# A ring of eight x buffers, three weighting buffers and PSUM sums in the column loop of a long convolution with expert choice

## The chip, the cores and the metric

The kernel runs on one core of a Trainium2 chip. The metric is the device time of one execution in microseconds, the median of several runs.

## The reference

The first part is a long causal convolution per channel, computed by a discrete Fourier transform of length 2S; the second gives 128 tokens of each batch to a small two-layer network.

```python
B, S, D = 4, 12608, 128
h = (maximum(pos_emb @ w1, 0) @ w2) * exp(-0.01 * arange(S))[:, None]
u = x * v
y = irfft(rfft(u, 2*S, axis=1) * rfft(h, 2*S, axis=0), 2*S, axis=1)[:, :S]
a = x * y                                        # (B, S, D)
scores = einsum('bsd,d->bs', a, w_gate)
out = a.copy()
for b in range(B):
    idx = argpartition(-scores[b], 128)[:128]    # the 128 largest scores
    ye = maximum(a[b, idx] @ moe_w1, 0) @ moe_w2 # D -> 1024 -> D
    out[b, idx] += sigmoid(scores[b, idx])[:, None] * ye
```

## The kernel before

**Pipeline.** The transform of length 23114 = 91 x 254 is done by matmuls in stages. For each batch there are 32 groups of four channels; one iteration `t` of the main loop (line 1093) works on one group in several stages of delay: `load_u` and `load_h` (SyncE) load its inputs, `stage_u` (GpSimd, line 262) forms x * v, `f_s1` and `dft` (TensorE, lines 450 and 281) transform it, with copies by ScalarE (line 452 to `te`, line 284 to `qs`), `f_v`, `f_u`, `f_m`, `f_y` (VectorE, lines 456 to 471) multiply the spectra, `f_sd` (GpSimd) folds, and three iterations later `f_i` (TensorE, line 276) transforms half way back; ScalarE copies its result to `big` (lines 501, 502). Each engine works through its instructions in the order in which the program issues them, and all ordinary DMAs go through SyncE's one queue in that order. Waits are put in where two instructions touch the same data.

**Column loop.** When all 32 groups of a batch are in `big`, `P1.run` (line 632) makes the outputs of that batch: 127 columns of 128 positions by 128 channels, in 16 blocks of up to 8 columns, in the order `ORD`. i is a block's place in that order. A block is two half-blocks of four columns, h = 0 to 31. For each half-block:

- `mm` (lines 567, 571): TensorE makes four columns of the convolution in one PSUM bank, from a ring of four.
- `fin` (line 582): VectorE multiplies them with the block's x and writes the result over x, in SBUF.
- `weigh` (line 616): the result times the gate weights goes to a buffer ("room") of 4 x 128 columns. Half-blocks of the far blocks are weighted by GpSimd in two rooms of its own (`CE`), the other 20 by VectorE in rooms taken in turn. The weights for VectorE are a copy in the first bank of `bank2[1]`.
- `sums` (line 626): ScalarE sums each column of a room with a copy in place and an accumulator; this is the gate score. The sums of h >= 28 are left for later, except in the last batch.
- After the second half: the block's result is stored to HBM from the buffer of x (line 605), and the next x is loaded (line 544) into the buffer of the block before this one, whose store must have landed.

The buffers of x are seven places of 8 x 128 columns, block i in place i % 7. Places 0 to 4 are `xa` buffers, loaded in halves during the last groups of the batch (`LA`, line 1154). Places 5 and 6 are `XE[0]` and `XE[1]`, which lie over buffers of the pipeline that are idle during the loop; they are loaded at the loop's start (line 640). `XE[0]` begins at `qs` and covers both `qs` buffers and part of `mt`; `XE[1]` lies over `ws` and the start of the first `yz` buffer. The rooms of VectorE are two `wx` buffers, an idle `te` buffer and an idle `ht` buffer (`sd` in the last loop).

After the loop `f_i` and `dft` of the next iteration run; `dft` ends with ScalarE's copy to `qs`, and ScalarE's copies for `te` come right behind it. The selection of the 128 tokens (`topk_one`) runs in hooks of the next batch's iterations. After the fourth loop nothing covers it: the last selection and the last expert run follow.

Before the first loop the `xa` buffers are cleared by ScalarE, two in each of the first iterations (line 1111), since rows of x outside the sequence are not loaded. `gap` (line 209) is room at the end of PSUM banks for masks and small results.

Of the kernel before, what the change touches and what calls it, by code (L numbers as in the profile page):

```python
# [11 lines left out]
AF = mybir.ActivationFunctionType  # L12
# [5 lines left out]
B, S, D, FO = 4, 12608, 128, 64  # L18
# [5 lines left out]
NG = 32  # L24
HC = 4 * N1
# [4 lines left out]
HB = 4  # L30
# [7 lines left out]
NU, NV, NX, NH = 4, 2, 5, 3  # L38
# [2 lines left out]
PJ = (N3 + 1) // 2  # L41
NC, CO = 4, 2
NE = 3
LA = range(32 - 12, 32 - 2)
NS, ND = 66, 4
NWARM = 8
JB = 9
# [7 lines left out]
OFF, _o = {}, 0  # L55
# [3 lines left out]
    _o += _k * _w  # L59
ARENA = _o  # L60
XE = [OFF["qs"][0] + k * 12 * D for k in range(2)]
CE = [o + 8 * D for o in XE]
POS0, HID0 = 0, PJ * N1

# [109 lines left out]
def hyena_moe(ctx, tc, xg, x2, pos, bw, ww, wg, mw1, mw2, fo, fc, c1, gx, cf, ci, wm, tk, out):  # L174
# [18 lines left out]
    def buf(name, k, shape):  # L193
        o, n, w = OFF[name]
        return view(arena, o + (k + (name == "yz")) % n * w, shape)
# [11 lines left out]
        return view(bank2[k], 0, shape)  # L207

    def gap(k, n):
        return bank2[k].rearrange("p (c x) -> p c x", c=2)[:, :, HC:HC + n]  # L210

    def c3(a):
        return a.rearrange("p (c x) -> p c x", c=2)
# [312 lines left out]
    class P1:  # L526
# [10 lines left out]
        def load_a(self, i, a=0, z=8):  # L537
            if i < len(ORD):
                k = ORD[i]
                j0, j1 = blocks[k]  # L540
                z = min(z, j1 - j0)
                o = i % (NX + len(XE))
                self.xa[k] = buf("xa", o, [128, 8, D]) if o < NX else view(arena, XE[o - NX], [128, 8, D])
                nc.sync.dma_start(self.xa[k][P0:P0 + PR, a:z], x2[self.b, :, j0 + a:j0 + z])

        def comb(self):
# [27 lines left out]
        def fin(self, h):  # L574
            ja, n = self.hbs[h]
            blk = ja // 8
            xa = self.xa[blk]
            js = slice(ja % 8, ja % 8 + n)
            end = self.last and h >= len(self.hbs) - 2
            if end:  # L580
                self.weigh()
            nc.vector.tensor_tensor(out=xa[:, js], in0=self.s4.pop(h)[:, :n], in1=xa[:, js], op=ALU.mult)  # L582
            if not end:
                self.weigh()
                far = ja >= JM and h + 1 < len(self.hbs) and h not in DW
                if h >= NL and not self.last:
                    o = OFF["cm"][0] + 2 * NC * D if h < 30 else OFF["wx"][0]
                    wx = view(arena, o + h % 2 * HB * D, [128, HB, D])
                elif far:
                    wx = view(arena, CE[self.pw % 2], [128, HB, D])  # L590
                    self.pw += 1
                else:
                    wx = view(arena, self.wx[self.nw % 4], [128, HB, D])
                    self.nw += 1
                self.mul = xa[:, js], wx[:, :n], ja, n, far, h
                if far:
                    self.weigh()
            else:
                for k in range(n):
                    nc.vector.scalar_tensor_tensor(out=junk, in0=xa[:, ja % 8 + k], scalar=1.0,  # L600
                                                   in1=self.wg, op0=ALU.mult, op1=ALU.mult,
                                                   accum_out=self.sc[:, ja + k:ja + k + 1])
            if ja + n == blocks[blk][1]:
                j0, j1 = blocks[blk]
                nc.sync.dma_start(out[self.b, :, j0:j1], xa[P0:P0 + PR, :j1 - j0])
                i = ORD.index(blk)
                if i:
                    self.load_a(i - 1 + NX + len(XE))
                if blk in CB:
                    self.comb()  # L610

        def weigh(self):
            if self.mul:
                x, wx, ja, n, far, h = self.mul
                eng, w = (nc.gpsimd, wgb) if far else (nc.vector, self.wg)
                eng.tensor_tensor(out=wx, in0=x, in1=w.unsqueeze(1).to_broadcast([128, n, D]), op=ALU.mult)  # L616
                cols = [(wx[:, k], ja + k) for k in range(n)]
                if h < NL or self.last:
                    self.sums(cols)
                else:  # L620
                    self.late += cols
            self.mul = None

        def sums(self, cols):
            for x, j in cols:
                nc.scalar.activation(out=x, in_=x, func=AF.Copy, accum_out=self.sc[:, j:j + 1])  # L626

        def mask(self):
            sc, m = (self.sc, negm) if self.last else (c3(self.sc), negp)
# [2 lines left out]
        def run(self, ex):  # L632
            self.last = ex is not None
            self.ring = (0, 1, 2) if ex else (3, 2, 0, 1)
            self.wx = [OFF["wx"][0], OFF["wx"][0] + HB * D, OFF["te"][0] + (2 * HC if ex else 0),
                       OFF["sd"][0] if ex else OFF["ht"][0] + ((self.b + 1) * NG + 2) % NH * 2 * HC]
            self.wg = ps2(1, [128, D], f"wg_{self.b}")
            nc.scalar.copy(out=self.wg, in_=wgb)
            for k in range(len(XE)):
                self.load_a(NX + k)  # L640
            for k in range(2):
                self.comb()
            for h in range(len(self.hbs)):
# [449 lines left out]
    for t in range(NT + LAG):  # L1093
# [4 lines left out]
        if t < NT:  # L1098
# [9 lines left out]
            spare[0] = None  # L1108
            bg.hook("w", 1)
            load_u(t + NU)  # L1110
            for k in range(2 * t, min(2 * t + 2, NX)):
                nc.scalar.activation(out=buf("xa", k, [128, 8 * D]), in_=one.to_broadcast([128, 8 * D]), func=AF.Copy,
                                     scale=0.0)
            if t == 2:
                nc.scalar.copy(out=negp, in_=c3(negm))
# [99 lines left out]
```

## Time and profile before

| | us |
|---|---|
| median of 3 runs (lowest, highest) | 869.85 (867.72, 872.17) |
| the profiled execution | 872.12 |
| its span, first to last instruction | 870.3 |
| TensorE matmuls busy in it | 833.4 (96%) |
| VectorE busy | 750.5 (86%) |
| GpSimd busy | 720.1 (83%) |
| ScalarE busy | 626.3 (72%) |

The granted TensorE clock is 0.99 of full speed. Busy shares are means over stages with different limits: a wait counts where it is the last to end. In the rows PE is TensorE, DVE VectorE, ACT ScalarE, POOL GpSimd, SP SyncE; `a` and `c` are PSUM banks, `arena` the SBUF area of most buffers, `big` the transformed groups, `out_dram` the output.

### The profile page before, as it was taken

How to read it: one execution, taken by the hardware profiler on the slowest of the kernel's cores; microseconds unless marked ns; L12 is line 12 of the kernel's file. 1: busy time of each engine (PE TensorE's matmuls, PEld its weight loads, DVE VectorE, ACT ScalarE, POOL GpSimd, SP SyncE). 2: the span in 40 equal slices, each digit the busy share in tenths (PEclk: the TensorE clock that was granted, in tenths of full speed). 3: DMA queues.
4: the chain of work that ended last, by engine and by line, in shares of the span. 5: the costliest groups of instructions: out<-in, count | busy, mean ns of one | idle time of the engine just before them, and what ended most of it. 6: DMA issues, size and time to landing. Idle time of an engine off the chain costs nothing.

```text
span 870.3 us, 45948 instructions
## 1 busy us (share of the span) xinstructions
PE 833.4 (96%) x19382; PEld 684.6 (79%) x19382; DVE 750.5 (86%) x1498; ACT 626.3 (72%) x2291; POOL 720.1 (83%) x837
## 2 busy tenths in 40 slices
PE   8999999999999999999998999999999999999875
PEld 5766668888889777778897777778996777779864
DVE  7978789999999799999996998999978989997873
ACT  6665575555559879885597898965797989657961
POOL 5799659999999689998997798989977989889610
PEclk9999999999999999999999999999999999999987
DMA  7044587677878977688789767788788767857810
GB/s 255 9 168 173 189 296 235 219 220 233 273 224 277 310 215 214 210 235 253 229 242 298 243 202 221 225 257 249 207 278 284 216 198 237 239 153 211 297 45 7
DMA packets 83278, 190.32 MB, mean 219 GB/s; under 512 B 9699, under 2 KB 46668, under 8 KB 83072
## 3 DMA queue, kind: packets, MB, share of 16 engines
q1 hardware_dynamic: 82816, 186.86, 68.5%
q8 instruction: 152, 2.49, 1.2%
q0 software_dynamic: 256, 0.52, 0.2%
q14 instruction: 54, 0.44, 0.1%
HBM read 147.63 MB, written 39.71 MB: 215 GB/s over the span
## 4 chain that ended last, share of the span: by engine, by line
PE 71%; DVE 14%; DMA 7%; ACT 5%; issue 2%; POOL 0%; POOLq 0%; DVEq 0%; ACTq 0%; SPq 0%
PE c L276 20%; PE c L281 15%; PE a L450 15%; DMA out_dram<-arena 5%; ACT arena L626 3%; PE c L571 3%; PE a L567 3%; PE a L397 3%; PE c L397 2%; PE a L571 2%; PE c L422 2%; PE c L567 2%; DVE big L365 2%; DMA arena<-in_x_dram 2%; DVE arena L464 1%
## 5 line engine op out<-in xcount | busy, mean ns | idle before, releaser
L276 PE MATMUL c<-ci_sb,arena 128*23 128x128 f32 x8128 | 250.0, 273 | 6.6 <-issue 3.2
L276 PEld LDWEIGHTS c<-ci_sb,arena 128*23 128x23 f32 x8128 | 227.7, 103 | 16.3 <-issue 7.0
L281 PE MATMUL c<-arena,cf_sb 128*32 128x364 f32 x2048 | 183.5, 470 | 7.0 <-ACT arena L452 4.6
L450 PE MATMUL a<-cons,arena 128*32 128x182 f32 (+1 forms) x4096 | 185.5, 318 | 0.7 <-DVE arena L582 0.5
L450 PEld LDWEIGHTS a<-cons,arena 128*32 128x32 f32 (+1 forms) x4096 | 137.2, 110 | 45.1 <-issue 11.2
L501 ACT COPY big<-c 128x800 f32<-128x800 f32 x127 | 103.8, 818 | 81.8 <-PE c L276 81.4
L626 ACT ACTIVATE arena<-arena 128x128 f32<-128x128 f32 x504 | 148.0, 299 | 11.5 <-DVE arena L616 11.4
L477 POOL TENSOR_TENSOR arena<-arena 128x364 f32<-128x364 f32 x127 | 113.8, 896 | 49.4 <-DVE arena L471 41.4
L452 ACT COPY arena<-a 128x364 f32<-128x364 f32 x256 | 119.5, 467 | 42.1 <-PE a L450 36.9
L262 POOL TENSOR_TENSOR arena<-arena 128x508 f32<-128x508 f32 x128 | 139.1, 1087 | 9.0 <-DMA arena<-in_xg_dram 9.0
L464 DVE TENSOR_TENSOR arena<-c,arena 128x728 f32<-128x728 f32 x127 | 116.3, 915 | 3.8
L465 DVE TENSOR_TENSOR c<-c,arena 128x728 f32<-128x728 f32 x127 | 116.1, 915 | 0.0
L478 POOL TENSOR_TENSOR arena<-arena 128x364 f32<-128x364 f32 x127 | 114.3, 900 | 0.0
L281 PEld LDWEIGHTS c<-arena,cf_sb 128*32 128x32 f32 x2048 | 69.3, 110 | 52.5 <-issue 31.6
L626 ACT ACTIVATION_READ_ACCUMULATOR arena<-arena 128x1 f32 x504 | 96.3, 191 | 0.0
L459 DVE TENSOR_TENSOR c<-c,arena 128x364 f32<-128x364 f32 x128 | 69.6, 544 | 23.6 <-ACT arena L284 21.0
L521 POOL TENSOR_TENSOR big<-big,arena 128x224 f32<-128x224 f32 x128 | 74.4, 581 | 10.0
L554 POOL TENSOR_TENSOR arena<-big 128x512 f32<-128x512 f32 x64 | 80.0, 1284 | 0.7 <-PE a L567 0.3
L470 DVE TENSOR_TENSOR arena<-c,arena 128x364 f32<-128x364 f32 x127 | 68.3, 537 | 12.8
L284 ACT COPY arena<-c 128x364 f32<-128x364 f32 x128 | 59.1, 462 | 26.1 <-DMA out_dram<-arena 9.1
L520 POOL TENSOR_TENSOR big<-big,arena 128x224 f32<-128x224 f32 x128 | 74.5, 582 | 0.0
L456 DVE TENSOR_TENSOR c<-c,arena 128x364 f32<-128x364 f32 x128 | 69.6, 544 | 2.6
(222 smaller groups left out, 1374.0 us busy)
## 6 DMA issues: line engine op xcount, KB each, us to landing
arena<-in_xg_dram SPq DMA_DIRECT2D x256, 254.0 KB, 3.5
arena<-hd SPq DMA_DIRECT2D x128, 364.0 KB, 4.2
out_dram<-arena SPq DMA_DIRECT2D x64, 420.0 KB, 6.0
arena<-in_x_dram SPq DMA_DIRECT2D x44, 420.0 KB, 5.0
hd<-arena SPq DMA_DIRECT2D x32, 364.0 KB, 2.4
arena<-in_x_dram SPq DMA_DIRECT2D x40, 210.0 KB, 4.8
arena<-in_pos_dram SPq DMA_DIRECT2D x16, 182.0 KB, 3.9
arena<-in_moe_w_dram SPq DMA_DIRECT2D x2, 512.0 KB, 6.0
```

What stands on the lines that cost most here:

```text
L262: nc.gpsimd.tensor_tensor(out=x, in0=x, in1=v, op=ALU.mult)
L276: nc.tensor.matmul(o[32 * k:32 * k + c.stop - c.start], lhsT=lhsT[:, c], rhs=rhs, start=True, stop=True)
L281: nc.tensor.matmul(pq[w][a:a + 32], lhsT=cf_sb[:, 2 * w + a // NQ, a % NQ:a % NQ + 32], rhs=te[:, a // NQ], start=True, stop=True)
L450: nc.tensor.matmul(tps[s // 2][c, s % 2], lhsT=u[:, s, c], rhs=c1_sb[:, k], start=True, stop=True)
L452: nc.scalar.copy(out=te[:, :, 2 * h:2 * h + 2].rearrange("p e s i -> p s e i"), in_=tps[h])
L464: nc.vector.tensor_tensor(out=mt, in0=uv, in1=ht[:, 0].unsqueeze(1).to_broadcast([128, 2, HC]), op=ALU.mult)
L465: nc.vector.tensor_tensor(out=uv, in0=uv, in1=ht[:, 1].unsqueeze(1).to_broadcast([128, 2, HC]), op=ALU.mult)
L477: eng.tensor_tensor(out=nat(sd[:, 0]), in0=nat(yz[:, 0]), in1=rev(yz[:, 1]), op=ALU.add)
L478: eng.tensor_tensor(out=nat(sd[:, 1]), in0=rev(yz[:, 0]), in1=nat(yz[:, 1]), op=ALU.subtract)
L501: nc.scalar.copy(out=ay[:, t % NG, :NJ + JM, ss], in_=o3[:, :, :NJ + JM].rearrange("p s x -> p x s"))
L554: nc.gpsimd.tensor_tensor(out=cm[:, e].rearrange("p j (g s) -> p j g s", s=4), in0=av[0], in1=av[1], op=op)
L626: nc.scalar.activation(out=x, in_=x, func=AF.Copy, accum_out=self.sc[:, j:j + 1])
```

## The change

Places: an eighth one is added, over the two `wx` buffers, and comes first in the list `XP`; the `xa` buffers follow, then `XE[0]` and `XE[1]`. The first six are loaded in halves during the last groups, two iterations earlier than before, and are cleared at the start. VectorE's rooms are now three: the idle `te` buffer, the second bank of `bank2[1]` in PSUM, and the idle `ht` (or `sd`) buffer. The sums over the room in PSUM write their products to a piece of SBUF behind the `te` room. To free that bank, the gaps are contiguous columns of the first bank.

```diff
-LA = range(32 - 12, 32 - 2)
+LA = range(32 - 14, 32 - 2)
...
+XP = [OFF["wx"][0], *(OFF["xa"][0] + k * 8 * D for k in range(NX)), *XE]
+NP0 = NX + 1
...
     def gap(k, n):
-        return bank2[k].rearrange("p (c x) -> p c x", c=2)[:, :, HC:HC + n]
+        return bank2[k][:, HC:HC + 2 * n].rearrange("p (c x) -> p c x", c=2)
...
-                o = i % (NX + len(XE))
-                self.xa[k] = buf("xa", o, [128, 8, D]) if o < NX else view(arena, XE[o - NX], [128, 8, D])
+                self.xa[k] = view(arena, XP[i % len(XP)], [128, 8, D])
...
-                    wx = view(arena, self.wx[self.nw % 4], [128, HB, D])
+                    wx = self.wx[self.nw % 3]
...
                 if i:
-                    self.load_a(i - 1 + NX + len(XE))
+                    self.load_a(i - 1 + len(XP))
...
-                cols = [(wx[:, k], ja + k) for k in range(n)]
+                cols = [(wx[:, k], wx[:, k] if wx.tensor is arena.tensor else self.sums_o, ja + k) for k in range(n)]
...
-            for x, j in cols:
-                nc.scalar.activation(out=x, in_=x, func=AF.Copy, accum_out=self.sc[:, j:j + 1])
+            for x, o, j in cols:
+                nc.scalar.activation(out=o, in_=x, func=AF.Copy, accum_out=self.sc[:, j:j + 1])
...
-            self.wx = [OFF["wx"][0], OFF["wx"][0] + HB * D, OFF["te"][0] + (2 * HC if ex else 0),
-                       OFF["sd"][0] if ex else OFF["ht"][0] + ((self.b + 1) * NG + 2) % NH * 2 * HC]
+            o = OFF["te"][0] + (2 * HC if ex else 0), OFF["sd"][0] if ex else OFF["ht"][0] + ((self.b + 1) * NG + 2) % NH * 2 * HC
+            self.wx = [view(arena, o[0], [128, HB, D]), view(bank2[1], 512, [128, HB, D]), view(arena, o[1], [128, HB, D])]
+            self.sums_o = view(arena, o[0] + HB * D, [128, D])
...
             for k in range(len(XE)):
-                self.load_a(NX + k)
+                self.load_a(NP0 + k)
...
-            for k in range(2 * t, min(2 * t + 2, NX)):
-                nc.scalar.activation(out=buf("xa", k, [128, 8 * D]), in_=one.to_broadcast([128, 8 * D]), func=AF.Copy,
+            for k in range(2 * t, min(2 * t + 2, NP0)):
+                nc.scalar.activation(out=view(arena, XP[k], [128, 8 * D]), in_=one.to_broadcast([128, 8 * D]), func=AF.Copy,
                                      scale=0.0)
```

## Rows read from the trace of the kernel before

**Rows 1.** The page, part 1: busy time, share of the span, instructions.

```profile
PE 833.4 (96%) x19382; PEld 684.6 (79%) x19382; DVE 750.5 (86%) x1498; ACT 626.3 (72%) x2291; POOL 720.1 (83%) x837
```

**Rows 2.** Windows of loops 1 to 3: length, each engine's busy time, clock, DMA share, GB/s.

```profile
254.21:291.04 36.83, 36.83 (x676) 36.66 (x672) 32.66 (x53) 32.36 (x218) 34.40 (x31) 1.00 0.83 253
432.37:470.53 38.16, 37.26 (x673) 36.62 (x672) 31.92 (x52) 32.81 (x219) 34.77 (x32) 1.00 0.83 249
612.33:650.75 38.42, 37.34 (x675) 36.62 (x672) 32.01 (x52) 32.84 (x219) 34.01 (x31) 1.00 0.79 240
```

**Rows 3.** Lines 582 and 284, whole span: until what they waited, us, times.

```profile
  DMA arena<-in_x_dram: 9.9, 11
...
  DMA out_dram<-arena: 9.1, 3
```

**Rows 4.** Timeline of PE at the ends of loops 1 and 2: start, us, [idle before].

```profile
289.20 1.92 PE L567 MATMUL a<-big,cons 128*64 128x128 f32 x32
...
478.57 0.82 PE L281 MATMUL c<-arena,cf_sb 128*32 128x364 f32 x8 [1.56 <-ACT arena L452]
```

**Rows 5.** The chain that ended last, in order of time: start, us, what.

```profile
289.25 7.36 DMA out_dram<-arena
...
469.06 8.03 DMA out_dram<-arena
...
649.27 7.41 DMA out_dram<-arena
```

**Rows 6.** Timeline of SP at the end of loop 2: issues of loads and stores.

```profile
464.88 0.34 SPq L544 DMA_DIRECT2D arena<-in_x_dram  x1
465.26 0.40 SPq L605 DMA_DIRECT2D out_dram<-arena  x1
467.75 0.34 SPq L544 DMA_DIRECT2D arena<-in_x_dram  x1
468.14 7.34 SPq L605 DMA_DIRECT2D out_dram<-arena  x6
```

**Rows 7.** Windows at the ends of loops 1 to 3; the last column is GB/s.

```profile
291.00:296.61 5.61, 5.45 (x151) 4.18 (x152) 3.03 (x5) 2.46 (x12) 2.89 (x4) 1.00 0.95 361
286.25:296.61 10.36, 10.20 (x238) 8.80 (x238) 6.43 (x11) 7.21 (x44) 5.97 (x6) 1.00 0.94 322
466.38:477.09 10.71, 9.60 (x230) 7.45 (x226) 6.35 (x10) 5.45 (x32) 6.99 (x7) 1.00 0.90 314
471.00:477.09 6.09, 5.89 (x168) 4.37 (x157) 3.25 (x6) 1.71 (x7) 3.76 (x4) 1.00 0.95 354
646.11:656.68 10.57, 9.12 (x206) 6.91 (x206) 6.35 (x10) 6.20 (x37) 5.98 (x6) 1.00 0.94 322
651.00:656.68 5.68, 5.31 (x148) 3.83 (x141) 3.47 (x6) 1.93 (x8) 2.85 (x4) 1.00 0.94 354
```

**Rows 8.** The page, part 6: stores, KB each, median us from issue to landing.

```profile
out_dram<-arena SPq DMA_DIRECT2D x64, 420.0 KB, 6.0
```

**Rows 9.** DMA view, 284 to 300 us: GB/s in 40 slices of 0.4 us.

```profile
GB/s 113 164 215 399 379 379 338 205 154 287 328 379 379 410 215 123 174 256 348 379 389 379 399 348 389 389 348 358 379 328 318 389 328 266 287 292 281 281 305 316
```

**Rows 10.** Timeline of DVE near the end of the last loop.

```profile
823.47 0.69 DVE L582 TENSOR_TENSOR arena<-a,arena 128x512 f32<-128x512 f32 x1 [0.48 <-DMA arena<-in_x_dram]
```

**Rows 11.** Line 626 in loop 1 (ns min/median/max, first and last start); timeline of DVE.

```profile
L626 ACT ACTIVATE arena<-arena x112: 292/294/312, 259.4 to 292.0; 128x128 f32<-128x128 f32 x112
...
282.58 0.68 DVE L616 TENSOR_TENSOR arena<-arena,c 128x512 f32<-128x512 f32 x1
```

**Rows 12.** Groups by line: count | busy us, mean ns | idle before.

```profile
L464 DVE TENSOR_TENSOR arena<-c,arena 128x728 f32<-128x728 f32 x127 | 116.3, 915 | 3.8
L465 DVE TENSOR_TENSOR c<-c,arena 128x728 f32<-128x728 f32 x127 | 116.1, 915 | 0.0
...
L502 ACT COPY arena<-a 128x112 f32<-128x112 f32 x2 | 0.5, 265 | 0.0
```

**Rows 13.** Groups by line: the fills at the start.

```profile
L1112 ACT ACTIVATE arena<-cons 128x1024 f32<-128x1024 f32 x5 | 5.1, 1054 | 0.0
```

**Rows 14.** Timeline of DVE after loop 1.

```profile
300.26 0.54 DVE L470 TENSOR_TENSOR arena<-c,arena 128x364 f32<-128x364 f32 x1
```

## The prediction

> **What bounds the kernel now.** I read the page first: TensorE is busy 96% of the span, so it sets the time wherever it is not made to wait [rows 1]. Four times the spectral pipeline stops for a column loop, one per batch. By windows from a loop's first matmul to the pipeline's next, TensorE has no gap in the first loop (36.83 us); the second and third take 38.16 and 38.42 us for the same work, 1.3 and 1.6 us more [rows 2]. Then the waits. VectorE's multiplication by x (line 582) waited 11 times, 9.9 us in all, for a load of x; ScalarE's copy to `qs` (line 284), the first use of that buffer after a loop, waited three times, 9.1 us in all, for a store [rows 3]. These are the two waits that the change touches.
>
> Which of them ends last? After the second loop TensorE sat 1.56 us until line 452, the copy right behind line 284 on ScalarE [rows 4]. The chain says why: each seam (the passage from a loop back to the pipeline) is on a store that lands at 289.25 + 7.36 = 296.61, at 477.09 and at 656.68 us [rows 5]. It is the third of the six stores at the end of a loop, that of block i = 12. That block lies at `XE[0]`, which covers both `qs` buffers. From that landing ScalarE's copies, and then TensorE, follow at a fixed distance. So what the change is worth at a seam is read from the time at which the store from `XE[0]` lands, not from line 582.
>
> **Places and loads.** With seven places block i sits in place i % 7; `XE[0]` is place 5 and its last block is i = 12. With eight, `XE[0]` is place 6 and its last block is **i = 14**. Ahead of the loop eight blocks are loaded, not seven, and in it eight, not nine. SyncE's order stays: store i, a load that must wait until store i - 1 has landed, store i + 1. So those eight loads are issued when they were, and each brings a block that is needed one block later. In the second loop the eighth load is issued at 464.88, store 9 at 465.26, the ninth load at 467.75, and the last six stores are queued behind it [rows 6]. The ninth is gone after the change: stores 10 to 12, long ready, follow store 9 at once, 13 and 14 as VectorE finishes.
>
> The waits at line 582 shrink, and TensorE gets back the 1.3 and 1.6 us inside loops 2 and 3. It comes to the seam that much earlier, and there it waits for line 452, unless the store lands earlier too. What is late next is the `XE[0]` store, and its cost is a sum of bytes.
>
> **The seam, in bytes.** From 1.5 us after the eighth load's issue to the landing, the queue moved 10.36 x 322 = 3336 kB in loop 1, 10.71 x 314 = 3363 in loop 2 and 10.57 x 322 = 3404 in loop 3 [rows 7]. After the change one load is gone from this stretch and two stores (13, 14) have joined: one transfer more, 430 kB (420 KB on the page) [rows 8]. The rate rises, since SyncE no longer holds the queue empty: where stores were queued it was 361, 354 and 354 GB/s [rows 7]. I take those, as the tail will consist of queued stores:
> - loop 1: 3766 / 361 = 10.43 us, +0.07;
> - loop 2: 3793 / 354 = 10.71 us, 0.00;
> - loop 3: 3834 / 354 = 10.83 us, +0.26.
>
> Sum **+0.3 us**. Upper end: the rate stays at the stretch's mean (322, 314, 322): 11.70, 12.08 and 11.91 us, +4.0 in all. Lower end: 373 GB/s, the mean of the ten slices from the nineteenth on in the tail of loop 1 [rows 9]: 11393 / 373 = 30.5 us against 31.6, -1.1.
>
> **The last loop** has no `qs` copy behind it. There the multiplication of the last block waited 0.48 us for its load, on the way to the final selection [rows 10]. That block now comes with the eighth load, some 2 us earlier: **-0.5 us** (ends 0, and -0.7 if another short wait for a load in this loop goes too).
>
> **The other edits.** *Three rooms for four.* A room is free when ScalarE has summed it. The sums of loop 1 run without a gap, 112 columns from 259.4 to 292.3 us, 293 ns each [rows 11]. The tightest reuse is half-block 21, written from 282.58 on [rows 11], whose room held half-block 18: 19 x 4 columns x 0.293 = 22.3 us after 259.4, so 281.7. It fits by 0.9 us: 0, covered by that slack. Without it VectorE would wait there, hold the PSUM ring and TensorE behind it; but the first 2 us of that would lie under the `qs` wait.
>
> *One room in PSUM.* VectorE's product costs 915 ns into SBUF and 915 ns into PSUM where size and sources are the same [rows 12]: 0. A sum with a PSUM source has no row. The nearest is a copy of 112 columns out of PSUM, 265 ns [rows 12], against 294 for a sum of 128 [rows 11]: between -29 and, turned round, +29 ns on 6 x 4 columns, 0.7 us of ScalarE a loop either way. ScalarE ends its sums at 292.3, has two copies to make and then stands at `qs` until 296.6: 0. The Trainium skill (Perfetto Trace Analysis, "Optimizing Scalar/DVE Operations") gives a fixed cost of some 60 ns for VectorE on SBUF and 125 on PSUM, and of 93 and 51 for ScalarE; by it the six products would cost VectorE an estimated 0.4 us more and the sums ScalarE 1.0 us less per loop. The equal 915 ns do not bear out the first, and the total would be the same, since both lie under the `qs` wait.
>
> *Output of these sums, gaps.* They write one SBUF buffer on one engine in order, and the gaps hold as many elements in one bank as in two: 0. *Zero fill.* One more fill of 1.05 us on ScalarE [rows 13] while the pipeline starts, before all engines are loaded: 0, at worst its own 1.05. *Two more half loads ahead of each loop*: the same bytes earlier, where SyncE is idle between its issues: 0.
>
> *A new neighbour.* `XE[1]` now holds the last block, and its store must land before line 470 writes `yz` at 300.26 [rows 14]. It lands one transfer (430 kB at 361, 1.2 us) after the store from `XE[0]`, near 298: 0, with 2 us to spare.
>
> **Sum**: +0.3 - 0.5 = -0.2 us. On the profiled execution that is 872.12 - 0.2 = 871.9; that execution (its span and 1.8 us around it) lies at the upper end of the runs shown (867.72 to 872.17), 2.3 us above their median. On the median 869.85 it gives **869.6 us**.
>
> **Rivals.** *Faster: the last stores are bound by latency, not by bytes.* Then the `XE[0]` store lands 6.0 us (the page's median) after its block is done [rows 8]. In loop 1 TensorE ends half-block 29 at 289.2 [rows 4], 35.0 us into the loop; VectorE adds 0.7: 295.9, -0.7. The same distance in loops 2 and 3 gives 474.1 and 654.0: -3.0 and -2.7. With the last loop -6.9: **863 us**. For it: loops 2 and 3 have lost time that TensorE gets back. Against: 3793 kB would have to pass from 466.4 to 474.1, 490 GB/s, and no slice shows over 410 [rows 9]. A gain over 0.5% in all needs 11393 kB in 27.8 us, 410 GB/s throughout. The Trainium skill (DMA: Bandwidth & Descriptors, "Bandwidth") measured a lone core near 425; by that the seams would gain an estimated 4.8 us and the kernel 5.3. The 354 to 361 of a full tail [rows 7] speak against it.
>
> *Slower: the tail does not run full, with two stores more ahead of `qs`.* Place: the `XE[0]` store at each seam. At the mean rates of the loops, 253, 249 and 240 GB/s [rows 2], it lands 4.5, 4.5 and 5.4 us later: +14.5, with the last loop +14.0, **884 us**. It is over 0.5% from 312 GB/s down. Against: those means come with a queue that a waiting load kept short.
>
> *The change does not do what it says*: block 15 comes as late as before. Then the -0.5 is gone: 870.2 us.
>
> **How the numbers follow.** About 0.5% (4.35 us) is what can be told from no change here. Forecast case 0.68, the change without effect 0.08, faster rival 0.14, slower rival 0.10. Of the forecast case 0.03 reaches beyond 0.5% on the fast side and 0.01 on the slow one: the store landed 42.4, 44.7 and 44.4 us into the three loops [rows 2, 5], a spread of 2 us for the same code, and each seam can come out that way. Faster 0.17, same 0.72, slower 0.11. The forecast's own ends are -1.8 and +4.0 us, 868.0 to 873.9; with the spread of the runs (867.7 to 872.2) and a part of the faster rival the range is 864.5 to 874.0. It leaves out 0.09 at either end.
>
> **What would show it.** Right: waits of line 582 for loads that hold TensorE gone, and 36.8 us in all three windows of rows 2; line 284 waiting three times for a store, 9 to 13 us in all; that store the sixth of seven in a row, landing within 0.6 us of 42.4, 44.7 and 44.4 us into the loop; no wait of VectorE for ScalarE at line 616; near 355 GB/s in the tail. Wrong: line 284 waiting under 6 us in all (the faster rival), the store landing over a microsecond later at under 320 GB/s (the slower one), or line 470 waiting for a store.

## The result and the profile after

The changed kernel takes **877.12 us** (median of 19 runs, 870.08 to 883.75) where the kernel before takes 868.94 beside it (19 runs): 1.0093 times as long, 95% interval 1.0077 to 1.0109, so 6.7 to 9.5 us more. The forecast was 869.6 (864.5 to 874.0) with 0.72 on no change; it was wrong.

The profiled execution after took 878.10 us, its span 876.3. Lines of the code are one or two higher than before: the multiplication by x is 583, the weighing 617, the sums 627, the copy to `qs` 286, `f_i` 278. The page's first part answers to [rows 1], and windows of all four loops, from their first matmul to the next work of TensorE, to [rows 2]:

```profile
PE 831.4 (95%) x19382; PEld 685.9 (78%) x19382; DVE 748.2 (85%) x1498; ACT 632.4 (72%) x2292; POOL 719.7 (82%) x837
```

```profile
254.07:293.99 39.92, 37.28 (x676) 36.62 (x672) 31.82 (x52) 32.60 (x209) 34.05 (x31) 1.00 0.84 266
432.60:472.51 39.91, 37.27 (x675) 36.62 (x672) 31.90 (x52) 32.61 (x209) 34.29 (x32) 1.00 0.80 254
614.62:654.53 39.91, 37.28 (x675) 36.62 (x673) 31.82 (x52) 32.60 (x209) 34.18 (x31) 1.00 0.84 263
787.68:828.62 40.94, 37.92 (x674) 36.86 (x675) 29.97 (x54) 33.18 (x215) 33.32 (x31) 1.00 0.78 247
```

Of the engines only ScalarE is busier than before, by 6.1 us in the whole span, but every loop is 39.9 us long, the last 40.94 (37.26 before). The two waits that the change was aimed at did shrink: line 583 waits for no load at all, and line 286 once for a store, 1.8 us (9.1 us in [rows 3]). In their place stands a new one. What the weighing of all engines waited for, and its groups with the sums:

```profile
its engine sat idle before it (us, times) until:
  ACT arena L627: 34.4, 29
```

```profile
L617 DVE TENSOR_TENSOR arena<-arena,c 128x512 f32<-128x512 f32 x55 | 37.5, 683 | 30.8 <-ACT arena L627 30.6
L617 DVE TENSOR_TENSOR c<-arena,c 128x512 f32<-128x512 f32 x24 | 16.5, 686 | 0.0
...
L627 ACT ACTIVATE arena<-arena 128x128 f32<-128x128 f32 x408 | 120.0, 298 | 18.5 <-DVE arena L617 18.5
...
L627 ACT ACTIVATE arena<-c 128x128 f32<-128x128 f32 x96 | 26.2, 273 | 2.3
```

Before, line 616 on VectorE had waited 0.3 us in all. Now the products that go to SBUF wait 30.6 us for ScalarE, those that go to the PSUM room (`c<-arena,c`) never. The timeline of one turn of the rooms in loop 1 shows how:

```profile
270.38 0.69 DVE L617 TENSOR_TENSOR c<-arena,c 128x512 f32<-128x512 f32 x1
...
270.98 0.69 DVE L583 TENSOR_TENSOR arena<-c,arena 128x512 f32<-128x512 f32 x1
...
272.53 0.27 ACT L627 ACTIVATE arena<-c 128x128 f32<-128x128 f32 x1
...
272.92 0.28 ACT L627 ACTIVATE arena<-c 128x128 f32<-128x128 f32 x1
...
273.32 0.28 ACT L627 ACTIVATE arena<-c 128x128 f32<-128x128 f32 x1
...
273.72 0.28 ACT L627 ACTIVATE arena<-c 128x128 f32<-128x128 f32 x1
...
274.12 0.69 DVE L617 TENSOR_TENSOR arena<-arena,c 128x512 f32<-128x512 f32 x1 [2.46 <-ACT arena L627]
274.73 0.68 DVE L583 TENSOR_TENSOR arena<-c,arena 128x512 f32<-128x512 f32 x1
...
275.46 1.09 PE L568 MATMUL c<-big,cons 128*64 128x128 f32 x16 [1.08 <-DVE arena L583]
```

Two things are to be seen. **The wait.** VectorE writes the PSUM room at 270.38. Its next weighing has its inputs and a free room in SBUF, yet starts only at 274.12, when the fourth sum over the PSUM room is done. What that product shares with those sums is the PSUM tile: the weights are its first bank, the room its second. The multiplication behind it waits too, the ring stays full, and TensorE stops. It is a wait on a semaphore and not a slower access: the longest semaphore wait of VectorE at line 617 lasts 1665 ns, at line 616 before 21 ns, while the products take as long as before. **The pitch.** The four sums begin 0.40 us apart, though one takes 0.27; sums in place begin 0.293 apart [rows 11]. They all write `sums_o`, and each waits for the one before it (run e8 below). 24 columns a loop make 24 x 0.107 = 2.6 us of ScalarE, all in the time for which VectorE waits. In the last loop the chain of waits runs along ScalarE (the shares of this window by line):

```profile
by line: ACT arena L627 71.3%; PE a L572 8.3%; DVE arena L617 7.8%; issue 5.3%; DVE arena L583 2.9%; DVE arena L601 2.7%; ACT big L503 1.2%; ACT arena L967 0.4%; PE a L278 0.3%; DVEq L583 0.1%; DVEq L617 0.1%; DVEq L601 0.0%
```

**Where the time went.** Both kernels were profiled twice (the second time in the runs g1 and g2). Stretches from the timeline, in us; a seam ends at the sixth `f_i`:

| | before | before again | after | after again |
|---|---|---|---|---|
| start to the first loop | 254.21 | 254.00 | 254.07 | 255.47 |
| loops 1 to 3 with their seams | 186.55 | 184.78 | 187.21 | 185.97 |
| pipeline between them | 344.51 | 344.11 | 346.40 | 345.42 |
| last loop | 37.26 | 37.26 | 40.94 | 40.94 |
| after it | 47.81 | 48.71 | 47.71 | 49.66 |
| span | 870.34 | 868.86 | 876.33 | 877.46 |

The last loop costs 3.68 us each time. Loops 1 to 3 are 3.1, 1.7 and 1.5 us longer in the first pair, yet with their seams they lose 0.7 us together (1.2 in the second pair): TensorE comes later to a wait that was there anyway. How much of the loss this covers is not fixed: a seam of the kernel before differs by up to 2.1 us between its two profiles, and in the run f3, whose loops 1 to 3 are those of the changed kernel, loops and seams take 191.2 us (that execution, 877.49 us, was the longest of its twelve). The start of the pipeline, its first `f_s1`, lies anywhere from 106.4 to 108.6 us in the traces but e5's (108.3 and 108.1 before, 106.7 and 108.6 after), which hides a small constant loss there. In its timeline ScalarE makes two fills in the iteration from 118.53, and TensorE waits behind them:

```profile
118.53 2.00 ACT L1114 ACTIVATE arena<-cons 128x1024 f32<-128x1024 f32 x2
...
120.83 1.42 PE L452 MATMUL a<-cons,arena 128*32 128x182 f32 x32
122.06 1.93 PE L278 MATMUL c<-ci_sb,arena 128*23 128x128 f32 x64
124.86 1.43 PE L283 MATMUL c<-arena,cf_sb 128*32 128x364 f32 x16 [0.87 <-DVE arena L473]
126.08 1.14 PE L452 MATMUL a<-cons,arena 128*32 128x182 f32 x24
```

From one `f_s1` (line 452) to the next it is 5.25 us here. In the kernel before, and in every run with its five fills, that iteration takes 4.3: the sixth fill makes it 0.95 us longer. From the first `f_s1` to the first loop it is 145.9 us in both profiles before, 147.4 and 146.9 after. The three shares make 5.3 us in the first pair and 5.8 in the second, of the 8.1 measured; the spans of the two pairs differ by 6.0 and 8.6 us.

### The profile page after: what moved, and what is told of

Read it like the earlier page. It is cut to its first block, busy times and chain, and to the rows that moved or that the text cites. A ratio compares the mean times of both kernels' runs of the same rounds, so it can differ in the third digit from the quotient of the medians.

```text
span 876.3 us, 45966 instructions
## 1 busy us (share of the span) xinstructions
PE 831.4 (95%) x19382; PEld 685.9 (78%) x19382; DVE 748.2 (85%) x1498; ACT 632.4 (72%) x2292; POOL 719.7 (82%) x837
## 4 chain that ended last, share of the span: by engine, by line
PE 64%; DVE 15%; ACT 14%; issue 4%; DMA 2%; POOL 0%; POOLq 0%; DVEq 0%; ACTq 0%
PE c L278 21%; PE c L283 16%; PE a L452 15%; ACT arena L627 12%; PE a L399 3%; PE c L399 2%; PE c L424 2%; DVE arena L466 2%; DVE c L467 2%; DVE c L458 1%; DVE big L367 1%; DVE c L461 1%; DMA out_dram<-arena 1%; PE c L419 1%; DVE arena L617 1%
## 5 line engine op out<-in xcount | busy, mean ns | idle before, releaser
L627 ACT ACTIVATE arena<-arena 128x128 f32<-128x128 f32 x408 | 120.0, 298 | 18.5 <-DVE arena L617 18.5
L461 DVE TENSOR_TENSOR c<-c,arena 128x364 f32<-128x364 f32 x128 | 69.6, 544 | 25.2 <-ACT arena L286 22.0
L627 ACT ACTIVATION_READ_ACCUMULATOR arena<-arena 128x1 f32 x408 | 77.2, 189 | 0.0
L286 ACT COPY arena<-c 128x364 f32<-128x364 f32 x128 | 59.1, 462 | 19.9 <-PE c L283 7.4
L617 POOL TENSOR_TENSOR arena<-arena,wgb 128x512 f32<-128x512 f32 x47 | 51.2, 1094 | 26.6 <-DVE arena L583 20.9
```

The source lines that it names most:

```text
L627: nc.scalar.activation(out=o, in_=x, func=AF.Copy, accum_out=self.sc[:, j:j + 1])
```

## The experiments

All ratios are to the kernel before, run on the same chip beside them. Theory at the outset: the two waits. Rivals: the eight places, or PSUM as such.

**e1_in_place**, meant to take the second wait away:

```diff
-cols = [(wx[:, k], wx[:, k] if wx.tensor is arena.tensor else self.sums_o, ja + k) for k in range(n)]
+cols = [(wx[:, k], wx[:, k], ja + k) for k in range(n)]
```

> The changed kernel, with the sums of the PSUM room written in place as the others are. Theory (the loss is made inside the loops by two waits: VectorE's next weighing waits until ScalarE has summed the PSUM room, and each of those sums waits for the one before it because all write one buffer): this takes only the second away. 24 sums a loop at 0.106 us less give ScalarE 2.5 us back per loop; VectorE's waits at its weighing fall from 8.3 to some 4 to 6 us a loop, TensorE's gaps from 2.6 to 0.5 to 1.5 us, and the time to 871 to 874 us (877.1 changed, 868.9 before). Rival (the eight places and their earlier loads cost the time, the waits are slack): still 876 to 878, with the gaps unchanged. Second rival (the shared output is all of it): 869.

876.8 us, 1.0091 (1.0065 to 1.0117). It did not do what it was to do: in place in PSUM each sum still waits for the one before, 0.40 us apart, although they touch different columns. That again the whole tile is what is waited for would explain it; no run shows that. The sum itself got shorter for nothing, and VectorE's wait stayed:

```profile
L627 ACT ACTIVATE c<-c 128x128 f32<-128x128 f32 x96 | 25.0, 261 | 2.3
```

**e2_weights_sbuf** and **e3_both** (with e1's edit) take the weights out of the tile:

```diff
-self.wg = ps2(1, [128, D], f"wg_{self.b}")
-nc.scalar.copy(out=self.wg, in_=wgb)
+self.wg = wgb
```

> The changed kernel, with VectorE's weights read from their SBUF copy and not from the first bank of the tile whose second bank is the PSUM room. Theory: VectorE's waits for ScalarE at its weighing (8.3, 8.1, 8.3 and 5.9 us in the four loops) go, TensorE's gaps fall from 2.6 to under 0.3 us a loop, the last loop from 40.9 to about 37.3 us, and the time to 869 to 870 us; ScalarE's sums stay 2.5 us a loop longer, and lie under the waits at the seams. Unknown: what a product with both sources in SBUF costs VectorE (0.915 us with the weights in PSUM); over 1.0 us it would hold TensorE and give 871 or more. Rival (places and loads): 876 to 878.

> Both edits on the changed kernel: no wait that the PSUM room brings, eight places kept. Theory: 868 to 869.5 us, as before or some tenths under it, sums at a pitch of 0.27 to 0.29 us. Rival (eight places cost the time): 876 to 878, as changed. If it comes out over 871 with no gap in TensorE inside the loops, a third cause is at work at the seams.

884.84 us, 1.0171 (1.0144 to 1.0199), and 885.02, 1.0184 (1.0158 to 1.0211). The wait all but went (1.4 to 2.7 us in loops 1 to 3), and a dearer price came, in e2's groups:

```profile
L617 DVE TENSOR_TENSOR arena<-arena,wgb 128x512 f32<-128x512 f32 x55 | 53.8, 978 | 6.2 <-ACT arena L627 6.1
...
L617 DVE TENSOR_TENSOR c<-arena,wgb 128x512 f32<-128x512 f32 x24 | 25.4, 1059 | 0.0
L617 POOL TENSOR_TENSOR arena<-arena,wgb 128x512 f32<-128x512 f32 x47 | 66.0, 1421 | 3.7 <-DVE arena L583 2.2 <-ACT arena L627 1.6
```

With both sources in SBUF VectorE's product takes 0.98 to 1.06 us in the mean, not 0.68, and GpSimd's 1.42, not 1.09. It is not the sources alone, as single products show (ns: shortest, median, longest):

```profile
L617 DVE TENSOR_TENSOR arena<-arena,wgb x55: 676/924/1792, 257.9 to 834.8; 128x512 f32<-128x512 f32 x55
L617 POOL TENSOR_TENSOR arena<-arena,wgb x47: 1083/1536/1613, 261.9 to 833.7; 128x512 f32<-128x512 f32 x47
```

The shortest on either engine are as fast as with the weights in PSUM, and the five products of GpSimd during which VectorE weighs nothing take 1084 to 1090 ns. The Trainium skill (SBUF — State Buffer, "Terms") has VectorE and GpSimd share a pair of SBUF ports; both engines' slowing agrees with it; that the loser is blocked for a whole instruction, as the page has it, would fit VectorE's longest product, 1792 ns, which is about its shortest and one of GpSimd's together, and is more than the means show. The two runs say nothing on the theory but that the weights must stay in PSUM.

**e4_rooms_alone**: the kernel before, seven places, with the change's `gap`, three rooms and `sums_o`.

> The kernel before with the three rooms alone (PSUM room, shared output, contiguous gaps), seven places. Theory: the same two waits as in the changed kernel, some 8 us of VectorE a loop, TensorE's gaps 2.6 us a loop, last loop 3.6 us longer; and the store ahead of the copy to the first buffer after each loop comes later with VectorE, with nothing gained at the seams, so 877 to 883 us, no better than the changed kernel. Rival (places and loads make the loss): 868 to 870.

875.29 us, 1.0071 (1.0046 to 1.0095), a little under the 877 to 883 expected: VectorE waits 8.3 us a loop for ScalarE in loops 1 to 3, TensorE's gaps are 2.6, the last loop 40.94. The rooms alone make most of the loss, and the rival that the eight places make it falls; what they add (1.0093 against 1.0071) is within the intervals.

**e5_last_loop_sbuf** and **f3_last_loop_fill** keep the PSUM room in loops 1 to 3; f3 also spreads the fills (as f1 below):

```diff
-self.wx = [view(arena, o[0], [128, HB, D]), view(bank2[1], 512, [128, HB, D]), view(arena, o[1], [128, HB, D])]
+mid = view(arena, o[1] + 2 * HC, [128, HB, D]) if ex else view(bank2[1], 512, [128, HB, D])
+self.wx = [view(arena, o[0], [128, HB, D]), mid, view(arena, o[1], [128, HB, D])]
```

> The changed kernel, with the PSUM room replaced in the last loop alone by an SBUF buffer that is idle there (the second of the two sd buffers); loops 1 to 3 keep it. Theory (VectorE's next weighing waits until ScalarE has read the PSUM room, because room and weights lie in one PSUM tile, and the last loop has nothing behind it that takes this up): VectorE's waits for ScalarE at the weighing in the last loop (5.9 us) go to under 1, TensorE's last loop falls from 40.9 to 37.3 us, the time by 3.6 to 873.5 us (872.5 to 874.5). Rival (three rooms are too few, wherever they lie): the loop stays at 40 to 41 us and the time at 877.

> The changed kernel with an SBUF buffer for the PSUM room in the last loop alone (as in the run e5) and the fills spread; loops 1 to 3 keep the PSUM room, its two waits and the places of the change. Theory: last loop 37.3 us, no wait of VectorE for ScalarE at its weighing there, the fifth f_s1 after 4.2 to 4.3 us; what is left are the seams at 0.2 us each: ratio 1.000 to 1.002. Rival (the waits in loops 1 to 3 cost more than the profile shows): 1.003 to 1.005.

873.59 us, 1.0029 (1.0006 to 1.0052), and 872.74, 1.0023 (1.0001 to 1.0045), just over its expected range. The loop is read in f3's trace, as the granted clock of e5's is 0.75. In f3 the last loop is that of the kernel before, to the hundredth:

```profile
791.96:829.22 37.26, 37.26 (x675) 36.92 (x675) 30.50 (x55) 32.39 (x220) 32.98 (x30) 1.00 0.79 249
```

So by the ratios the last loop holds 5.6 us of the loss (1.0093 less 1.0029), with the fill 6.1, and by the trace 3.7 and 4.6; the intervals of these differences reach 2.4 us to either side and let both be true.

**e6_weights_other_bank**: weights in another PSUM tile in loops 1 to 3, and **e7**, its control on the kernel before.

```diff
-self.ring = (0, 1, 2) if ex else (3, 2, 0, 1)
+self.ring = (0, 1, 2) if ex else (2, 0, 1)
...
-self.wg = ps2(1, [128, D], f"wg_{self.b}")
+self.wg = ps2(1 if ex else 2, [128, D], f"wg_{self.b}")
```

> The changed kernel, in loops 1 to 3 with VectorE's weights in a PSUM bank of another tile than the room; the ring of the convolution's columns has three banks there, as it has in the last loop. Theory: VectorE's waits for ScalarE at the weighing fall from 8.3 to under 1.5 us a loop, TensorE's gaps from 2.64 to under 0.5 and its loops from 39.7 to 37 to 37.5 us. What that gives at the seams is another matter: the store from the first place over the pipeline's buffers should then hold the copy to qs again, at 42.5 to 44.8 us into the loop, and the time is 873 to 877 us; if the seams get all of it, 869. Rival (the PSUM room costs by its accesses, not by a wait): loops stay at 39 to 40 us.

> Control: the kernel before with a ring of three banks in loops 1 to 3, nothing else. If a ring of three is enough, 868 to 870 us and loops of 36.8 to 38.4 us, and the ring of the run with the weights in another bank costs nothing; if VectorE's turn holds TensorE, its gaps inside the loops show it and the time is 871 or more.

e7: 871.76 us, 1.0016 (0.9988 to 1.0044); the smaller ring costs nothing that can be told in the time. In its trace the loops are 38.0, 38.8 and 39.8 us long, 1.2, 0.7 and 1.4 more than in [rows 2], so the ring by itself lengthens them and can't be what shortens e6's. e6: in loops 1 to 3 VectorE's waits fall from 8.3 to 0.4 us a loop, and TensorE makes its columns in 36.9 us without a gap, with the PSUM room and its sums 0.40 apart as they were. **That settles the first wait**: it is the shared tile, not the access. The time did not follow, 879.85 us, 1.0105 (1.0065 to 1.0144). `f_i` writes the tile to which the weights had been moved, so it waits for their last reader, three times (2.32, 2.59 and 2.35 us):

```profile
295.12 1.94 PE L278 MATMUL c<-ci_sb,arena 128*23 128x128 f32 x64 [2.32 <-DVE arena L617]
```

That gives back what the columns gained: up to `f_i` these loops take 39.2 to 39.5 us. With their seams they take 184.7 us in the profiled execution (875.04 us), no more than in the kernel before; what is slower there is the last loop, 40.96 us, which e6 leaves as it was, and the start with its fill. Five other executions took 876.5 to 882.9 at mean clocks of 0.984 to 0.986, and no trace shows where they lost the clock. The Trainium skill (PSUM — Partial Sum Buffer, "Specifications (TRN2)") says that ScalarE and VectorE can use PSUM side by side at full rate unless they meet in one bank. Room and weights lie in different banks, so by that rule the chip would not ask for the wait; no run has them in one tile without it.

**e8_two_outputs**: the second wait alone (column k of a room writes to `self.sums_o[k % 2]`).

```diff
-self.sums_o = view(arena, o[0] + HB * D, [128, D])
+self.sums_o = [view(arena, k + HB * D, [128, D]) for k in o]
```

> The changed kernel, with the sums of the PSUM room writing their products to two SBUF buffers in turn instead of one. Theory: the wait of each such sum for the one before goes, their pitch falls from 0.40 to 0.27 to 0.30 us, 2.4 us of ScalarE a loop; VectorE's waits for ScalarE shrink by up to 0.4 us per room, from 8.3 to about 6 us a loop, TensorE's loops by 0.5 to 2 us, the last loop by as much: 874 to 876 us. If the shared output has no part in the loss: 876 to 878, loops unchanged.

875.69 us, 1.0056 (1.0025 to 1.0087). Loop 1 and the last loop, in windows, are 2.2 us shorter, with VectorE's waits at 5.3 to 5.5 us in loops 1 to 3, 3.9 in the last:

```profile
253.35:291.10 37.75, 37.06 (x677) 36.62 (x674) 32.08 (x53) 31.02 (x213) 34.10 (x31) 1.00 0.81 260
...
785.38:824.17 38.79, 37.91 (x675) 36.86 (x675) 30.28 (x55) 31.61 (x218) 32.86 (x30) 1.00 0.80 255
```

So of the 3.68 us of the last loop 2.15 hang on the shared output and the other 1.53 on the tile; in loops 1 to 3 taking the tile's wait away takes both (e6). At the seams the gain was given back: line 286 waits for a store again, 2.8, 3.2 and 4.6 us.

**e9_no_waits**: both waits out everywhere (e5's and e8's edits; in loops 1 to 3 weights in bank 0, ring 3, 0, 1), eight places kept.

> The changed kernel without the waits that the PSUM room brought: in loops 1 to 3 the weights in the bank that the ring leaves free and that TensorE needs last after the loop (ring of three), two outputs in turn for the sums of the PSUM room; in the last loop an SBUF buffer for that room. Eight places kept as they are. Theory: TensorE's gaps inside the loops under 0.3 us, loops of 36.7 to 37.0 us, last loop 37.3; at the seams the copy to qs waits 2.5 to 4 us again for the store from the first place over the pipeline's buffers, as forecast, so the time is that of the kernel before within 2 us (ratio 0.998 to 1.002): the eighth place gives nothing. Rival (eight places are worth the 1.3 and 1.6 us of loops 2 and 3): ratio 0.996 or less.

871.54 us, 1.0036 (1.0011 to 1.0061), above the expected 0.998 to 1.002. This is the change without the waits that I had not forecast, with a ring of three, and it still gives nothing. Nor are its loops 36.7 to 37.0 us long. By windows:

```profile
255.06:292.28 37.22, 36.91 (x677) 36.67 (x673) 33.65 (x55) 32.59 (x225) 34.48 (x31) 1.00 0.83 264
433.85:471.79 37.94, 36.90 (x677) 36.66 (x673) 33.74 (x55) 33.20 (x226) 35.15 (x33) 1.00 0.83 258
613.87:652.39 38.52, 37.12 (x674) 36.64 (x672) 33.60 (x55) 32.85 (x226) 34.57 (x31) 1.00 0.80 252
```

Together that is 113.7 us, where [rows 2] have 113.4. In loops 2 and 3 VectorE still waits for late blocks of x (timeline), and TensorE waits for VectorE behind it, 1.04 us in loop 2 and 0.63 and 0.77 in loop 3:

```profile
471.05 0.69 DVE L583 TENSOR_TENSOR arena<-c,arena 128x512 f32<-128x512 f32 x1 [0.64 <-DMA arena<-in_x_dram]
...
649.79 1.29 DVE L583 TENSOR_TENSOR arena<-a,arena 128x512 f32<-128x512 f32 x2 [2.00 <-DMA arena<-in_x_dram]
```

Line 286 waits 3.5, 3.8 and 3.9 us. The chain at the first seam, and the stretches whose rate the forecast had taken as 361, 354 and 354 GB/s, by windows:

```profile
291.54 0.40 DVE arena L583
291.94 6.79 DMA out_dram<-arena
298.73 0.02 issue
298.75 0.04 ACTq L286
```

```profile
287.00:298.73 11.73, 11.32 (x268) 9.95 (x264) 6.44 (x11) 6.58 (x42) 8.23 (x9) 1.00 0.93 315
467.57:478.60 11.03, 9.53 (x236) 8.16 (x230) 4.74 (x8) 5.32 (x33) 7.45 (x9) 1.00 0.93 312
647.36:659.31 11.95, 10.19 (x240) 8.36 (x235) 4.86 (x8) 5.03 (x31) 7.67 (x9) 1.00 0.94 315
```

The store from `XE[0]`, that of block i = 14, goes out as soon as VectorE is done with its block and lands 6.2 to 6.8 us later, 43.7, 44.8 and 45.4 us into the loop (42.4, 44.7 and 44.4 before).

**e10_no_waits_places** (on e9), **e11_places** (on the changed kernel) and **e12_before_places** (on the kernel before, `XP[3:3] = XE` with seven) move the two places over the pipeline's buffers ahead, so that their last stores come earlier:

```diff
+XP = [OFF["wx"][0], *(OFF["xa"][0] + k * 8 * D for k in range(NX))]
+XP[4:4] = XE
+PRE = (0, 1, 2, 3, 6, 7)
...
-self.load_a(NP0 + k)
+self.load_a(4 + k)
...
```

> The run without waits, and the two places over the pipeline's buffers moved from the end of the eight to the middle: the one over both qs buffers takes blocks i = 4 and 12, not 6 and 14. Theory (each seam waits for the landing of that place's last store): the store of block 12 is issued with half-block 25, some 31 us into the loop, and lands by 38 us; the copy to qs waits for it no more, the sixth f_i comes 58 to 60 us into a loop, not 61.3 to 62.8, and the time falls 6 to 11 us under the kernel before (ratio 0.987 to 0.993). Rival (ScalarE's sums or the next store are right behind it): 0 to 3 us.

> The changed kernel with the places moved as in the run before this one, its room in PSUM and its waits left as they are. Theory: in the changed kernel the copy to qs waits only 0, 1.8 and 0.1 us for a store, since TensorE comes 3 us late; moving the places gains 0 to 2 us: 875 to 877. If it gains over 3 us, the store held more of the seam than the waits show.

> The kernel before (seven places, four rooms in SBUF) with the two places over the pipeline's buffers moved from fifth and sixth (counted from 0) to third and fourth: the one over qs takes blocks 3 and 10, not 5 and 12. Theory: the waits of 2.6, 3.6 and 2.9 us at the copy to qs go, the loops keep their 36.8 to 38.4 us, and the time falls by 5 to 9 us (ratio 0.990 to 0.994). Rival (something stands right behind that store: ScalarE's sums, the store from the other place): ratio over 0.997.

e10: 867.01 us, 0.9985 (0.9967 to 1.0003), 4.5 us under e9 but only 1.7 under the kernel before, with no change inside the interval: the rival's 0 to 3 us, not the 6 to 11 expected. The waits at line 287 fall to 0.4, 1.5 and 1.2 us, and the sixth `f_i` comes at 59.1, 60.9 and 60.4 us. e11: 875.76 us, 1.0073 (1.0042 to 1.0105), as expected. **e12: 865.15 us, 0.9963 (0.9940 to 0.9985): this beats both kernels**, by half of what I had expected. Its copy to `qs` waits for a store once, 0.7 us. A new wait takes a part back: with seven places the last blocks of x are late, now up to 3.40 us, and `f_i` waits behind them (second seam, timeline):

```profile
468.42 1.29 DVE L584 TENSOR_TENSOR arena<-c,arena 128x512 f32<-128x512 f32 x2 [3.40 <-DMA arena<-in_x_dram]
...
469.16 2.46 PE L279 MATMUL c<-ci_sb,arena 128*23 128x128 f32 x64 [2.61 <-DVE arena L584]
```

Where the gain of e12 lies, its one trace does not show: loops 1 to 3 with their seams take 185.5 us in it, the kernel before 186.6 and 184.8, and the second seam also has TensorE at half its clock (last section). In f4 below, with the same places, they take 182.5 us, in e10 180.4.

**f1_fill_spread** (on the changed kernel), **f2_no_waits_places_fill** (on e10), **f4_before_places_fill** (on e12): one fill in an iteration.

```diff
-for k in range(2 * t, min(2 * t + 2, NP0)):
+for k in range(t, min(t + 1, NP0)):
```

> The changed kernel, with the six fills of ScalarE at the start spread over six iterations, one in each, instead of two in each of three. Theory (the sixth fill makes the iteration in which it stands 0.95 us longer, since the pipeline has no slack for two fills of 1.05 us there): the fifth f_s1 follows the one before it by 4.2 to 4.3 us, not 5.25, and the time falls by 0.95 us, ratio to the kernel before 1.007 to 1.009. Rival (the pipeline takes that delay up later): no change, 1.009 to 1.010, the first loop beginning no earlier.

> The run without waits and with the places moved, fills spread too. Theory: 0.95 us less than without, ratio 0.996 to 0.998 where it was 0.9985, about 866 us. If the fill costs nothing it stays at 0.9985.

> The kernel before with its places moved (run e12) and its five fills spread one to an iteration. Theory: the fifth fill shared an iteration with nothing, and the two pairs before it stood where the pipeline still waits for other work, so 0 to 0.2 us: the ratio stays at 0.996.

877.2 us, 1.0093 (1.0061 to 1.0124); 868.51, 0.9985 (0.9960 to 1.0010); 868.19, 0.9970 (0.9942 to 0.9998). The trace of f1 shows the 0.95 us gone, 4.32 us from that `f_s1` to the next. The times can't tell 0.95 us; f1 and f2 came out as without the edit, as their rivals had it, and from the first `f_s1` to the first loop f1 takes 146.9 us, no less than g2. That the whole time pays for the fill is not shown.

**g1_before_again** and **g2_after_again**: both kernels once more, unchanged.

> The kernel before, unchanged, for a second profile. If its first profile was a slow one at the start, the first f_s1 begins at 106.5 us here, not 108.3, and the span is 866 to 868 us; if it was slow at the seams, the sixth f_i comes 60 to 61.5 us into a loop, not 61.3 to 62.8. The last loop is 37.3 us in either case; ratio 1.000.

> The changed kernel, unchanged, for a second profile: loops of 39.7 us, last loop 40.9, sixth f_i 61.5 to 63.5 us into a loop, 5.25 us between the fourth and the fifth f_s1; ratio 1.008 to 1.011.

871.41 us, 1.0019 (0.9995 to 1.0042), and 880.47, 1.0124 (1.0067 to 1.0181). The first profile was no worse than this at the start; the second seam of g1 is 2.1 us better (60.7 against 62.8), which is the spread of one seam. Everything expected of g2 but its ratio came, that lying higher.

## Why the prediction was wrong

**The step that failed** is the one on *Three rooms for four*: "It fits by 0.9 us: 0, covered by that slack." It asked when ScalarE frees a room that VectorE wants to write. The slack is real: in e9, with the same three rooms in loops 1 to 3, VectorE does not wait for a room. But the room moved into the tile from which VectorE reads the weights, and there a read had to wait for another engine's reads: 8.3 us a loop. I looked at who writes what, not at what lies beside it. The sign that I had named, a wait of VectorE for ScalarE at the weighing, is the one that came.

**A second step failed**: *Output of these sums*, "They write one SBUF buffer on one engine in order", put at 0. In order, but each behind the end of the one before: 24 x 0.107 us a loop. By itself it would have lain on ScalarE; it was paid since VectorE waited for ScalarE.

**A third**, which the first two hide in the changed kernel, is in *Places and loads*: "TensorE gets back the 1.3 and 1.6 us inside loops 2 and 3". In e9 these loops are 37.94 and 38.52 us long, 38.16 and 38.42 before: blocks of x still come 0.64 and 2.00 us late. That line 583 waits for no load in the changed kernel is no gain of the places, as VectorE comes later there. How much of e9's loops is due to its ring of three is not known.

**The cover was half right.** I wrote that a wait of VectorE would lie under the wait at `qs`. It did: loops 3.1, 1.7 and 1.5 us longer cost 0.7 and 1.2 us in all in the two pairs, which is less than the spread of one seam. The last loop has no seam, and I gave it only the 0.5 us of a load. There the two waits cost 3.68 us in full.

**The seam** went as forecast in its cause, not in its rate. The `XE[0]` store moved from i = 12 to i = 14 and held line 286 again once the loops were short (e9). The tail moved 312 to 315 GB/s, not 354 to 361, which is a little past the upper end of that term (314 to 322), and at two of three seams the store landed over 1 us later than before, the sign that I had given to the slower rival. e9's +3.1 us (1.0 to 5.3) fits that end with the fill, and it is near the slower rival's mechanism at a fifth of its price. The traces do not part the sum of bytes from a fixed time to land: the 6.2 to 6.8 us from the end of its block are near the faster rival's 6.0, but the block was done 36.9 us into loop 1, not 35.7. That an earlier block in `XE[0]` at the end does better is what e10 (block 12) shows against e9 (block 14).

**Other terms.** The product into PSUM costs the same (686 and 683 ns), the sum from PSUM 25 ns less: both as bounded. The zero fill was put at 0, "at worst its own 1.05"; it makes one iteration 0.95 us longer. Line 472 waits for no store, so the new neighbour cost nothing. The wait for the last block's load, put at -0.5 us, is gone in f3, but the stretch behind the last loop varies from 45.6 to 50.4 us between runs, so what it gave can't be told.

**What stays open**: 2.3 to 2.8 of the 8.1 us are in none of these three shares. The pipeline between the loops was 1.9 and 1.3 us longer after, and most of that is one delay in either profile, where `f_i` stops in its middle for nothing that the profile shows (`after` and g2, timeline):

```profile
562.13 0.52 PE L278 MATMUL c<-ci_sb,arena 128*23 128x128 f32 x11 [1.14 <-issue]
```

```profile
561.60 0.52 PE L278 MATMUL c<-ci_sb,arena 128*23 128x128 f32 x11 [0.61 <-issue]
```

Over the two iterations that it upsets it makes 1.95 and 1.15 us. f1, whose loops are the same, does not have it there, and the kernel before has such stops of up to 1.0 us at other places. What causes them, and whether the changed kernel has more of them, was not settled.

## What to carry to other kernels

A buffer moved into spare room brings its neighbours' dependencies along: in PSUM, ask which engine reads or writes anything else of the same tile, and put what two engines use at different paces in different tiles. A scratch output that nobody reads still orders its writers; give it two buffers. A wait costs what the stage behind it can't take up, so price it loop by loop, the last one apart; and where a store holds a buffer after a loop, move that buffer to an earlier place in the ring before adding places.

## What was not expected of the hardware

**TensorE's clock after a wait.** At e8's third seam TensorE stood idle for 2.66 us, and its next work ran at 0.50 of the clock, 1.2 GHz: 2.04 and 2.55 us for what takes 1.41, so the wait cost another 1.8. The timeline, and the window; then that of e12's second seam, after a wait of 2.61 us:

```profile
656.96 2.04 PE L283 MATMUL c<-arena,cf_sb 128*32 128x364 f32 x16 [2.66 <-ACT arena L454]
658.75 2.55 PE L452 MATMUL a<-cons,arena 128*32 128x182 f32 x32
...
662.87 1.40 PE L283 MATMUL c<-arena,cf_sb 128*32 128x364 f32 x16
664.10 1.41 PE L452 MATMUL a<-cons,arena 128*32 128x182 f32 x32
```

```profile
658.00:661.00 3.00, 3.00 (x40) 1.81 (x36) 2.68 (x6) 2.73 (x11) 0.81 (x1) 0.50 0.78 243
```

```profile
470.40:473.90 3.50, 3.50 (x48) 1.85 (x40) 2.57 (x4) 1.07 (x2) 2.51 (x3) 0.51 0.94 330
```

e6's three waits of 2.32, 2.59 and 2.35 us left the clock at 1.00 in its profiled execution; what decides between a wait of 2.59 us and one of 2.61 is not shown. Also unexpected: beside GpSimd's products, one PSUM source instead of two SBUF sources is worth 0.3 us of 0.98 to VectorE in the mean, and as much to GpSimd, which was not touched (e2).
